# Later batches of a delta-rule scan: each step multiplies by its triangular matrix M itself, and keys and queries are turned by products of 64x64 tiles

## The chip, the cores and the metric

The kernel runs on one core of a Trainium2 chip. The metric is the device time of one execution in microseconds (us); where several executions are shown, their median. Engines are named as in the profile: PE is TensorE's matmul, PEld its weight load, DVE is VectorE, ACT is ScalarE, POOL is GpSimd, SP is SyncE, which issues most DMAs.

## The reference: what is computed

A delta-rule attention runs over 768 time steps for 4 batches of 8 heads with 48 channels; its output, the heads laid side by side (384 channels), goes through a Fourier mixing and a two-layer MLP.

```
for t in range(S):                                   # per batch and head
    y[t]  = q[t] @ state
    v_old = state.T @ kn[t]                          # kn = k / (|k| + 1e-6)
    state = state + beta[t] * outer(kn[t], v[t] - v_old)
x = y, heads side by side                            # (4, 768, 384)
u = x + real(fft(fft(x, axis=seq), axis=channel))
out = u + relu(layernorm(u) @ w1) @ w2               # w1: 384 x 1536, w2: 1536 x 384
```

All of it is float32.

## The kernel before: tiling, staging and the order of the work

Time is cut into chunks of 64 (C). Within a chunk the recurrence is a unit triangular system, so with M the inverse of that triangle (with beta in it) a chunk needs only matrix products: U = M (V - K S), then S' = S + K^T U, and the output Q S + (masked Q K^T) U. Two chunks make a group g of 128 times (L); a batch has 6 groups (NL), the four batches 24. A step is step(g, c) for one chunk c of group g; a batch has 12 of them, one after the other through the state S, for all 8 heads at once.

What does not depend on S is prepared per group, in generators:

- pre_a(g) (line 263) loads a tile C of keys and transposes it to KT: four transposes of 128x128 with TensorE (helper tr, line 106, recorded as L107) into a PSUM tile "one", copied out by ACT (L272). Then the products of KT with itself, and two ACT copies, G and GX (L291, L293).
- invert(r) (line 297) inverts the 32x32 triangles of four groups at once, on DVE: 31 rounds of a multiply (L345) and an add (L349). A round r serves groups 4r to 4r+3.
- pre_q(g) (line 359) transposes the queries to QT in the same way (L371) and forms LQ, the masked product of keys and queries (L389).
- pre_m(g) (line 392) has three parts. POOL scales V by the key norms (L398) and lays out MT (L402), M transposed. Part one: products GX with M (32x32 tiles), ACT copies XM. Part two: products XM with M, ACT copies the last corner of MT (L426). Part three (lines 429 to 446): 16 products of MT with K, which give WT = (M K)^T, and 16 products of MT with V, which give U0 = M V; ACT copies both out (L442, L444).
- step(g, c) (line 448): 8 products of WT with S into a PSUM tile "pair"; DVE subtracts them from U0, which leaves U (L462); 8 products of K with U; DVE adds them to S (L481), which is the next state. With c = 1 it then makes the outputs of the group: 16 products of QT with the two states, copied by ACT (L502), and 16 products of LQ with U, added by DVE (L511).

The PSUM has two tiles "pair" (two banks each), two tiles "one" and two tiles "post" (one bank each), all in rings. In SBUF the rings that matter are V and MT (two each), K (three), and KT (seven, RING).

Batch 0's scan is written out in an order by hand (lines 700 to 775, inside manual_schedule). The scans of batches 1 to 3 (line 776 on) are not: there the program's order gives each instruction only its priority, and the scheduler of the framework puts ready instructions into each engine's queue. That program's order is made by run (line 644), which advances a list of generators by turns: first the step, then pre_q, pre_m and pre_a of later groups, the inversion (six pieces a turn), and then "side", the MLP of the batch before, two pieces a turn and four a step (beside, line 660). A piece of the MLP is three products for a block of hidden units (ph, L104, with a relu on DVE L619 or ACT L617) or four products for an output tile (po). What is left of the MLP after a scan runs beside the Fourier mixing (pf, pb) of the batch just scanned. The MLP of batch 3 has nothing beside it.

A step has a part up to each yield, so before the change: the WT products and the subtraction in the first turn, the K products and the addition in the second, the outputs in the third. The four MLP pieces of a step come in its first two turns.

All products go through mm (line 103, recorded as L104). In the profile one float32 product shows as two MATMUL records (8 calls of the K product are "x16"), a transpose by tr as one ("x4" for a tile).

Of the kernel before, what the change touches and what calls it, by code (L numbers as in the profile page):

```python
# [9 lines left out]
F32 = mybir.dt.float32  # L10
# [3 lines left out]
ALU = mybir.AluOpType  # L14
ACT = mybir.ActivationFunctionType

C = 64
# [41 lines left out]
def kernel(  # L59
# [10 lines left out]
    nc = tc.nc  # L70
# [23 lines left out]
    def ps_pair():  # L94
        return ps.tile([128, 2, 512], F32, tag="pair", bufs=2, name="pair")

    def ps_one():
        return ps.tile([128, 512], F32, tag="one", bufs=2, name="one")
# [4 lines left out]
    def mm(o, lhsT, rhs, start, stop=True):  # L103
        nc.tensor.matmul(o, lhsT=lhsT, rhs=rhs, start=start, stop=stop, skip_group_check=True)  # L104

    def tr(o, src, start):
        nc.tensor.matmul(o, lhsT=src, rhs=ident[0:src.shape[0], 0:src.shape[0]],  # L107
                         is_transpose=True, start=start, stop=True, skip_group_check=True)
# [148 lines left out]
    lo = [slice(64 * e, 64 * e + D) for e in range(2)]  # L257
    full = [slice(64 * e, 64 * e + 64) for e in range(2)]
    KTs, Gs, GXs, rounds, pre, xs = {}, {}, {}, {}, {}, {}
    S = {}  # L260
    SEQ = NL * L

    def pre_a(g):

        K = Cs[g % 3]
        r, li = divmod(g, RL)
        KT = KTs[g] = wk.tile([128, 2, 2, 128], F32, tag="KT", bufs=RING, name="KT")
        pt = ps_one()
        for i in range(4):
            tr(pt[:, 128 * i:128 * i + 128],  # L270
               K[:, 2 * i:2 * i + 2, :].rearrange("p h d -> p (h d)"), i == 0)
        nc.scalar.activation(KT.rearrange("p h j t -> p (h j t)"), pt, ACT.Copy)  # L272
        load_c(g + 3)
        yield
        if li == 0:
            Gs[r] = wk.tile([128, W, W], F32, tag="G", bufs=2, name="G")
        X = GXs[g] = wk.tile([128, 8, W], F32, tag="GX", bufs=8, name="GX")
        pg = ps_pair()
        for i in range(4):
            c, jj = divmod(i, 2)  # L280
            for q4 in range(4):
                for jp in range(2):
                    hh, blk = divmod(q4, 2)
                    t0 = c * C
                    rhs = KT[lo[jp], hh, jj, t0:t0 + C]
                    if blk:
                        rhs = rhs.rearrange("p (b t) -> p b t", b=2)[:, ::-1, :]
                    mm(pg[q4 * W:q4 * W + W, jp, C * i:C * i + C],
                       KT[lo[jp], hh, jj, t0 + blk * W:t0 + blk * W + W], rhs, i == 0)
        src = pg[:, :, 0:4 * C].rearrange("p a (i s) -> p a i s", s=C)  # L290
        nc.scalar.activation(Gs[r][:, 8 * li:8 * li + 8].rearrange("p (i a) s -> p a i s", a=2),  # L291
                             src[:, :, :, 0:W], ACT.Copy)
        nc.scalar.activation(X.rearrange("p (i a) s -> p a i s", a=2), src[:, :, :, W:C],  # L293
                             ACT.Copy)
        yield
# [62 lines left out]

    def pre_q(g, QT=None, LQ=None):

        Q, KT = Qs[g % 2], KTs.pop(g)
        early = QT is not None
        if QT is None:
            QT = wk.tile([128, 2, 2, 128], F32, tag="QT", bufs=2, name="QT")
            LQ = wk.tile([128, 2, 4, C], F32, tag="LQ", bufs=2, name="LQ")
        LQs[g] = (QT, LQ)
        pt = ps_one()
        for i in range(4):
            tr(pt[:, 128 * i:128 * i + 128],
               Q[:, 2 * i:2 * i + 2, :].rearrange("p h d -> p (h d)"), i == 0)  # L370
        nc.scalar.activation(QT.rearrange("p h j t -> p (h j t)"), pt, ACT.Copy)  # L371
        load_q(g + 2)
        yield
        pl = ps_pair()
        for i in range(4):
            c, jj = divmod(i, 2)
            for hh in range(2):
                for jp in range(2):
                    t0 = c * C
                    mm(pl[full[hh], jp, C * i:C * i + C], KT[lo[jp], hh, jj, t0:t0 + C],  # L380
                       QT[lo[jp], hh, jj, t0:t0 + C], i == 0)
        dst = LQ.rearrange("p c (jj jp) t -> p jp (c jj) t", jp=2)
        src = pl[:, :, 0:4 * C].rearrange("p a (i t) -> p a i t", t=C)
        mask = m_su[:, None, None, :].broadcast_to([128, 2, 4, C])
        if early:
            nc.scalar.activation(dst, src, ACT.Copy)
            nc.gpsimd.tensor_tensor(dst, dst, mask, op=ALU.mult)
        else:
            nc.vector.tensor_tensor(dst, src, mask, op=ALU.mult)  # L389
        yield  # L390

    def pre_m(g):

        r, li = divmod(g, RL)
        K, V, X = Ks[g % 3], Vs.pop(g), GXs.pop(g)
        MTd, Md, nT = rounds[r]
        m8 = slice(8 * li, 8 * li + 8)
        nc.gpsimd.tensor_tensor(V.rearrange("p c j d -> p (c j) d"),  # L398
                                V.rearrange("p c j d -> p (c j) d"),
                                nT[:, m8, None].broadcast_to([128, 8, D]), op=ALU.mult)  # L400
        MT = wk.tile([128, 8, 2, W], F32, tag="MT", bufs=2, name="MT")
        nc.gpsimd.tensor_tensor(MT, MTd[:, m8, None, :].broadcast_to([128, 8, 2, W]),  # L402
                                m_blk[:, None, :, None].broadcast_to([128, 8, 2, W]),
                                op=ALU.mult)

        px = ps_one()
        for m in range(8):
            for hh in range(2):
                r0 = 64 * hh
                mm(px[r0 + W:r0 + C, W * m:W * m + W], X[r0:r0 + W, m, :],  # L410
                   Md[r0:r0 + W, 8 * li + m, :], m == 0)
        XM = wk.tile([128, 8, W], F32, tag="XM", name="XM")
        for hh in range(2):
            rw = slice(64 * hh + W, 64 * hh + C)
            nc.scalar.activation(XM[rw].rearrange("p m s -> p (m s)"), px[rw, 0:8 * W],  # L415
                                 ACT.Copy, scale=-1.0)
        yield
        py = ps_one()
        for m in range(8):
            for hh in range(2):  # L420
                r0 = 64 * hh
                mm(py[r0:r0 + W, W * m:W * m + W], XM[r0 + W:r0 + C, m, :],
                   MTd[r0 + W:r0 + C, 8 * li + m, :], m == 0)
        for hh in range(2):
            rw = slice(64 * hh, 64 * hh + W)
            nc.scalar.activation(MT[rw, :, 1, :],  # L426
                                 py[rw, 0:8 * W].rearrange("p (m s) -> p m s", s=W), ACT.Copy)
        yield
        WT = wk.tile([128, 2, 2, 2, C], F32, tag="WT", bufs=2, name="WT")
        U0 = wk.tile([128, 2, 4, D], F32, tag="U0", bufs=2, name="U0")  # L430
        pw = ps_pair()
        pu = ps_one()
        for c in range(2):
            for j in range(4):
                for hh in range(2):
                    mt = MT[full[hh], 4 * c + j].rearrange("p b t -> p (b t)")
                    jj, jp = divmod(j, 2)
                    o = (2 * c + jj) * C
                    mm(pw[full[jp], hh, o:o + C], K[full[hh], 4 * c + j, :], mt, c == 0 and jj == 0)
                    o = (4 * c + j) * D  # L440
                    mm(pu[full[hh], o:o + D], mt, V[full[hh], c, j, :], c == 0 and j == 0)
        nc.scalar.activation(WT.rearrange("p h c j t -> p h (c j t)"), pw[:, :, 0:4 * C],  # L442
                             ACT.Copy)
        nc.scalar.activation(U0.rearrange("p c j d -> p (c j d)"), pu[:, 0:8 * D], ACT.Copy)  # L444
        pre[g] = (K, *LQs.pop(g), WT, U0)
        yield

    def step(g, c):

        b, n = divmod(g, NL)  # L450
        K, QT, LQ, WT, U0 = pre[g]
        begin = n == 0 and c == 0
        s0 = S.get((b, 2 * n + c))
        U = U0[:, c]
        if not begin:
            pw = ps_pair()
            for jj in range(2):
                for hh in range(2):
                    for jp in range(2):
                        mm(pw[full[hh], jp, D * jj:D * jj + D], WT[lo[jp], hh, c, jj, :],  # L460
                           s0[lo[jp], hh, jj, :], jj == 0)
            nc.vector.tensor_tensor(  # L462
                U.rearrange("p (jj jp) e -> p jp jj e", jp=2),
                U.rearrange("p (jj jp) e -> p jp jj e", jp=2),
                pw[:, :, 0:2 * D].rearrange("p a (j e) -> p a j e", e=D), op=ALU.subtract)
            yield
# [354 lines left out]
```

## Time and profile before

| | |
|---|---|
| eight runs | median 829.08 us, 817.48 to 832.37 |
| the profiled execution | 817.48 us, span of the instructions 815.6 us |
| busy in the span | PE 700.1 us, PEld 538.6, DVE 412.6, ACT 203.9, POOL 131.9 |
| batches 1 to 3 and their Fourier parts, 260 to 712 us | PE busy 428.54 of 452 us |
| last MLP, 712 to 816 us | PE busy 97.78 of 104 us |
| mean granted TensorE clock | 0.887 |

"PE busy" counts a matmul from its start to its modelled end, and neighbours overlap, so the cost of a block of products is best read from the start of its first record to the start of the next block's first. A line of the timeline gives the start in us from the span's start, the duration in us, engine, line, operation, output<-inputs, sizes (contraction x stationary columns, then output), and how many records are merged; in brackets, how long the engine was idle before and what released it.

### The profile page before, as it was taken

The numbers are of one execution on the slowest core, as the hardware profiler recorded it, in microseconds if no ns is written. First come the engines' busy times: TensorE is split into PE (matmuls) and PEld (weight loads), VectorE is DVE, ScalarE is ACT, GpSimd is POOL, SyncE is SP. The second block draws the span as 40 slices with busy tenths as digits, with TensorE's granted clock in tenths as the row PEclk, the third lists the DMA queues.
The fourth block names the chain that finished last, engine by engine and source line by source line (L and its number), as shares of the span: only waits on it lengthen the run. The fifth ranks groups of instructions, "written<-read, shape, count | busy, mean of one in ns | idle before, by whom it ended". The sixth has DMA issues, their size and how long they took to land.

```text
span 815.6 us, 23216 instructions
## 1 busy us (share of the span) xinstructions
PE 700.1 (86%) x10344; PEld 538.6 (66%) x10344; DVE 412.6 (51%) x1004; ACT 203.9 (25%) x470; POOL 131.9 (16%) x150
## 2 busy tenths in 40 slices
PE   5537565398888999899998898899999999899998
PEld 4426464387657767578866767677778677686774
DVE  1897757546997129926268414798122141611110
ACT  4312333163322422023312213212122121210010
POOL 6132135302311101132000102102000020100000
PEclk8555555596999999999998999999999999899999
DMA  9721144323300421112111122002010000000000
GB/s 133 210 44 27 32 104 111 94 42 86 114 16 21 75 52 34 23 31 55 32 37 31 21 45 46 12 10 46 17 45 17 11 12 1 19 1 20 10 10 19
DMA packets 107382, 36.06 MB, mean 44 GB/s; under 512 B 99633, under 2 KB 102930, under 8 KB 107282
## 3 DMA queue, kind: packets, MB, share of 16 engines
q1 hardware_dynamic: 105586, 33.50, 18.4%
q8 instruction: 81, 1.33, 0.7%
q0 software_dynamic: 512, 0.79, 0.6%
q10 hardware_dynamic: 1184, 0.30, 0.3%
q14 instruction: 19, 0.16, 0.1%
HBM read 29.84 MB, written 4.72 MB: 42 GB/s over the span
## 4 chain that ended last, share of the span: by engine, by line
PE 54%; DVE 30%; issue 5%; POOL 4%; ACT 3%; DMA 2%; SPq 1%; ACTq 0%; POOLq 0%; DVEq 0%
PE po L104 17%; PE ph L104 16%; PE pair L104 8%; DVE M L349 6%; DVE tmp L345 6%; PE one L104 5%; PE pf L104 3%; PE one L107 2%; PE pb L104 2%; DMA C<-in_k_dram 2%; POOL w L246 1%; DVE A L304 1%; DVE A L352 1%; DVE G L353 1%; DVE hT L619 1%
## 5 line engine op out<-in xcount | busy, mean ns | idle before, releaser
L104 PE MATMUL ph<-unT,w 128*128 128x256 f32 x864 | 209.2, 396 | 9.6 <-DVE hT L619 5.9
L104 PE MATMUL po<-w,hT 128*128 128x384 f32 x576 | 198.1, 496 | 5.6 <-POOL w L246 3.1
L104 PEld LDWEIGHTS ph<-unT,w 128*128 128x128 f32 x864 | 164.6, 196 | 37.7 <-DVE hT L619 9.1
L104 PEld LDWEIGHTS po<-w,hT 128*128 128x128 f32 x576 | 108.3, 192 | 74.0 <-POOL w L246 3.2
L619 DVE TENSOR_SCALAR hT<-ph 128x256 f32<-128x256 f32 x72 | 30.3, 421 | 109.6 <-PE ph L104 109.6
L349 DVE TENSOR_TENSOR M<-M,tmp 128x135 f32<-128x135 f32 (+15 forms) x186 | 71.5, 386 | 4.8
L345 DVE TENSOR_TENSOR tmp<-A,M 128x60 f32<-128x60 f32 (+15 forms) x186 | 69.5, 375 | 4.4
L617 ACT ACTIVATE hT<-ph 128x256 f32<-128x256 f32 x72 | 27.6, 384 | 145.4 <-PE ph L104 142.3
L629 DVE TENSOR_TENSOR x<-x,po 128x384 f32<-128x384 f32 x24 | 13.2, 551 | 97.3 <-PE po L104 97.2
L104 PE MATMUL one<-V,MT 64*64 64x48 f32 x768 | 47.4, 241 | 0.9 <-ACT MT L426 0.8
L402 POOL TENSOR_TENSOR MT<-A,pack 128x512 f32<-128x512 f32 x24 | 26.1, 1094 | 131.0 <-PE one L104 79.1
L398 POOL TENSOR_TENSOR V<-V,nT 128x384 f32<-128x384 f32 x24 | 20.8, 869 | 155.5 <-DMA V<-in_v_dram 55.1
L104 PEld LDWEIGHTS one<-V,MT 64*64 64x64 f32 x768 | 43.2, 159 | 2.8 <-ACT MT L426 1.7
L104 PE MATMUL pair<-MT,K 64*64 64x64 f32 x768 | 42.3, 256 | 1.6 <-ACT MT L426 1.0
L104 PE MATMUL pair<-S,WT 48*64 48x48 f32 x704 | 22.6, 245 | 21.7 <-DVE S L481 17.4
L104 PEld LDWEIGHTS pair<-MT,K 64*64 64x64 f32 x768 | 38.4, 151 | 3.2 <-ACT MT L426 1.6
L104 PEld LDWEIGHTS pair<-S,WT 48*64 48x64 f32 x704 | 16.7, 151 | 31.1 <-DVE S L481 18.6
L104 PEld LDWEIGHTS pair<-U,K 64*64 64x64 f32 x704 | 16.9, 151 | 30.4 <-DVE U L462 15.3
L104 PE MATMUL pair<-U,K 64*64 64x48 f32 x704 | 23.2, 246 | 15.4 <-DVE U L462 13.8
L481 DVE TENSOR_TENSOR S<-S,pair 128x192 f32<-128x192 f32 x40 | 14.0, 349 | 37.2 <-PE pair L104 37.2
L104 PE MATMUL one<-G,GX 32*32 32x32 f32 x768 | 19.0, 204 | 15.2 <-DVE G L353 15.2
L415 ACT ACTIVATE XM<-one 32x256 f32<-32x256 f32 x48 | 18.1, 376 | 54.6 <-PE one L104 53.6
(111 smaller groups left out, 923.4 us busy)
## 6 DMA issues: line engine op xcount, KB each, us to landing
w<-in_moe_w_ch_dram SPq DMA_DIRECT2D x12, 768.0 KB
Q<-in_q_dram SPq DMA_DIRECT2D x24, 192.0 KB
out_dram<-x SPq DMA_DIRECT2D x24, 192.0 KB
C<-in_k_dram SPq DMA_DIRECT2D x23, 192.0 KB
K<-in_k_dram SPq DMA_DIRECT2D x88, 48.0 KB
V<-in_v_dram SPq DMA_DIRECT2D x88, 48.0 KB
evt<-k_even SPq DMA_DIRECT2D x1, 579.0 KB
odt<-k_odd SPq DMA_DIRECT2D x1, 576.0 KB
```

The source lines that it names most:

```text
L104: nc.tensor.matmul(o, lhsT=lhsT, rhs=rhs, start=start, stop=stop, skip_group_check=True)
L107: nc.tensor.matmul(o, lhsT=src, rhs=ident[0:src.shape[0], 0:src.shape[0]], is_transpose=True, start=start, stop=True, skip_group_check=True)
L246: nc.gpsimd.tensor_tensor(dst, man.rearrange("p (c f) -> p c f", c=c), num.bitcast(F32).rearrange("p (c f) -> p c f", c=c), op=ALU.mult)
L345: nc.vector.tensor_tensor(t, A[:, j + 1:W, j:j + 1].broadcast_to([128, n, j + 1]), M[:, j:j + 1, 0:j + 1].broadcast_to([128, n, j + 1]), o ...
L349: nc.vector.tensor_tensor(M[:, j + 1:W, 0:j + 1], M[:, j + 1:W, 0:j + 1], t, op=ALU.add)
L398: nc.gpsimd.tensor_tensor(V.rearrange("p c j d -> p (c j) d"), V.rearrange("p c j d -> p (c j) d"), nT[:, m8, None].broadcast_to([128, 8, ...
L402: nc.gpsimd.tensor_tensor(MT, MTd[:, m8, None, :].broadcast_to([128, 8, 2, W]), m_blk[:, None, :, None].broadcast_to([128, 8, 2, W]), op=A ...
L415: nc.scalar.activation(XM[rw].rearrange("p m s -> p (m s)"), px[rw, 0:8 * W], ACT.Copy, scale=-1.0)
L481: nc.vector.tensor_tensor(s1v, s0.rearrange("p h j e -> p h (j e)"), pk, op=ALU.add)
L617: nc.scalar.activation(hT[:, fc, :], ph, ACT.Relu)
L619: nc.vector.tensor_scalar(hT[:, fc, :], ph, 0.0, None, op0=ALU.max)
L629: nc.vector.tensor_tensor(x[:, T, :], x[:, T, :], po, op=ALU.add)
```

## The change

Four things change, the first three only for batches 1 to 3 (groups 6 to 23).

1. pre_m ends after its second part: the 32 products of MT with K and V and the two ACT copies (WT, U0) are gone. What is handed to the step is MT and V.
2. A step of those batches multiplies KT with S (8 products, as many as WT with S before), DVE subtracts from V in place, then 8 products of MT with the difference give U in a PSUM tile "one", and ACT copies U out. Only then come the products of K with U. A step thus has one more turn: the four MLP pieces stand in the turns of KT S and of M, and K U with the addition stands in a third turn by itself.
3. KT, MT and V of a group are now read by the group's steps, so their ring buffers are held until the step of chunk 1 has read them.
4. For all 24 groups, keys and queries are turned by a new helper, turn: in place of four 128x128 transposes into "one", 16 plain products of 64x64 tiles with the identity into a "pair" (one bank for each half of the partitions), and one ACT copy of the same 512 elements a partition.

```diff
+    def turn(dst, src):
+
+        pt = ps_pair()
+        for i in range(4):
+            for c in range(2):
+                for jp in range(2):
+                    nc.tensor.matmul(pt[full[jp], c, C * i:C * i + C],
+                                     lhsT=src[full[c], 2 * i + jp, :], rhs=ident[full[c], full[c]],
+                                     start=i == 0, stop=True,
+                                     skip_group_check=True)
+        nc.scalar.activation(dst.rearrange("p h j (c t) -> p c (h j) t", c=2),
+                             pt[:, :, 0:4 * C].rearrange("p c (i t) -> p c i t", t=C), ACT.Copy)
...
-        pt = ps_one()
-        for i in range(4):
-            tr(pt[:, 128 * i:128 * i + 128],
-               K[:, 2 * i:2 * i + 2, :].rearrange("p h d -> p (h d)"), i == 0)
-        nc.scalar.activation(KT.rearrange("p h j t -> p (h j t)"), pt, ACT.Copy)
+        turn(KT, K)
...
-        Q, KT = Qs[g % 2], KTs.pop(g)
+        Q, KT = Qs[g % 2], KTs[g]
...
+        turn(QT, Q)
...
+        if g >= NL:
+            pre[g] = (K, *LQs.pop(g), MT, V)
+            yield
+            return
...
+        if b > 0:
+
+            if c == 0:
+                Us[0] = wk.tile([128, 2, 4, D], F32, tag="U0", bufs=2, name="U")
+            K, QT, LQ, MT, V = pre[g]
+            U0, KT = Us[0], KTs[g]
+            R, U = V[:, c], U0[:, c]
+            if not begin:
+                pw = ps_pair()
+                for jj in range(2):
+                    for hh in range(2):
+                        for jp in range(2):
+                            mm(pw[full[hh], jp, D * jj:D * jj + D],
+                               KT[lo[jp], hh, jj, c * C:c * C + C], s0[lo[jp], hh, jj, :], jj == 0)
+                R4 = R.rearrange("p (jj jp) e -> p jp jj e", jp=2)
+                nc.vector.tensor_tensor(
+                    R4, R4, pw[:, :, 0:2 * D].rearrange("p a (j e) -> p a j e", e=D),
+                    op=ALU.subtract)
+                yield
+            pu = ps_one()
+            for j in range(4):
+                for hh in range(2):
+                    mm(pu[full[hh], D * j:D * j + D],
+                       MT[full[hh], 4 * c + j].rearrange("p b t -> p (b t)"), R[full[hh], j, :],
+                       j == 0)
+            nc.scalar.activation(U.rearrange("p j e -> p (j e)"), pu[:, 0:4 * D], ACT.Copy)
+            yield
+        else:
+            K, QT, LQ, WT, U0 = pre[g]
+            U = U0[:, c]
+        if not begin and b == 0:
```

More of the change, by code (lines that the diff above doesn't have):

```diff
@@ L259 @@
     KTs, Gs, GXs, rounds, pre, xs = {}, {}, {}, {}, {}, {}
-    S = {}
+    S, Us = {}, {}
     SEQ = NL * L
+    def turn(dst, src):
[9 more added lines that the diff above has]
+                             pt[:, :, 0:4 * C].rearrange("p c (i t) -> p c i t", t=C), ACT.Copy)
     def pre_a(g):
@@ L366, in pre_q @@
         LQs[g] = (QT, LQ)
[L367 to L371, printed above, removed]
+        turn(QT, Q)
         load_q(g + 2)
@@ L450, in step @@
         b, n = divmod(g, NL)
-        K, QT, LQ, WT, U0 = pre[g]
         begin = n == 0 and c == 0
         s0 = S.get((b, 2 * n + c))
-        U = U0[:, c]
-        if not begin:
+        if b > 0:
[28 more added lines that the diff above has]
+        if not begin and b == 0:
             pw = ps_pair()
```

## The prediction

> **What bounds the kernel now.** I read the page first (engines, then the 40 slices), then the busy times by stage, then PE's timeline inside the stages, and last the waits of PE.
>
> ```profile
> PE 700.1 (86%) x10344; PEld 538.6 (66%) x10344; DVE 412.6 (51%) x1004; ACT 203.9 (25%) x470; POOL 131.9 (16%) x150
> PE   5537565398888999899998898899999999899998
> DVE  1897757546997129926268414798122141611110
> ```
>
> PE is low in the first third and at eight or nine tenths from slice 13 on (about 250 us): batches 1 to 3, where the change sits, are held mostly by PE. But DVE has three humps there. The busy times by stage (columns: length, then PE, PEld, DVE, ACT, POOL busy with counts, clock, DMA) separate them:
>
> ```profile
> 260.00:303.00 43.00, 42.60 (x986) 31.50 (x984) 6.63 (x16) 14.90 (x35) 4.73 (x6) 1.00 0.28 57
> 303.00:348.00 45.00, 38.79 (x573) 28.42 (x565) 42.34 (x109) 8.28 (x21) 7.63 (x8) 0.96 0.16 30
> ...
> 413.00:456.00 43.00, 38.59 (x549) 27.64 (x550) 37.13 (x96) 7.92 (x19) 3.95 (x5) 0.92 0.17 35
> ...
> 517.00:566.00 49.00, 44.88 (x358) 34.88 (x357) 44.96 (x127) 10.52 (x30) 4.78 (x8) 1.00 0.10 23
> 566.00:660.00 94.00, 92.98 (x1517) 68.50 (x1516) 20.61 (x47) 21.02 (x49) 7.58 (x8) 1.00 0.10 24
> ```
>
> Three stretches, 137 us together, belong to an inversion on DVE, with 4 to 6 us of PE idle in each: PE work saved there is no time. Between them PE is busy for 42.60 of 43 and 92.98 of 94 us. There each microsecond of PE work counts, and each wait that nothing fills. PE's timeline in the last stretch shows the repeating order:
>
> ```profile
> 610.42 0.45 PE L104 MATMUL pair<-U,K 64*64 64x48 f32 x16
> 612.23 2.86 PE L104 MATMUL ph<-unT,w 128*128 128x256 f32 x12
> 615.02 0.68 PE L104 MATMUL pair<-S,QT 48*64 48x48 f32 x32
> 615.52 0.65 PE L104 MATMUL pair<-U,LQ 64*64 64x48 f32 x32
> 616.31 0.45 PE L104 MATMUL pair<-S,WT 48*64 48x48 f32 x16
> 617.28 0.69 PE L104 MATMUL one<-G,GX 32*32 32x32 f32 x32
> 617.90 2.86 PE L104 MATMUL ph<-unT,w 128*128 128x256 f32 x12
> 620.69 0.45 PE L104 MATMUL pair<-U,K 64*64 64x48 f32 x16
> 620.96 0.66 PE L104 MATMUL pair<-QT,KT 48*64 48x64 f32 x32
> 621.55 2.86 PE L104 MATMUL ph<-unT,w 128*128 128x256 f32 x12
> 624.34 0.45 PE L104 MATMUL pair<-S,WT 48*64 48x48 f32 x16
> ```
>
> After the first product of each step (S,WT) and after its second (U,K) come two MLP pieces (ph, 2.8 us): DVE's subtraction or addition is done behind them, and PE waits for nothing. In PE's waits from 260 to 712 us the state (S L481) accounts for 2.0 us and U (L462) for 0.8 us.
>
> **The change part by part**, against the profiled execution's 817.48 us.
>
> 1. *Part three of pre_m goes.* Its 64 records run from 409.09 to 410.72 us, up to the next block: 1.63 us. Of the 18 groups, two (6 and 7) come before 260 us, where DVE holds the end (19.18 of 20 us busy from 240 to 260), and three of the other 16 fall into inversion stretches. 13 x 1.63 = -21.2 us. The ACT copies (0.60 + 0.48 us) were hidden behind PE, and so is their going.
>
> 2. *M in the step.* The new 8 products have the form of the MT,V products, 64x64 on 48 columns, and use only two of the four 64x64 places in the array. Where those ran apart from the MT,K products the trace has their price:
>
> ```profile
> 380.06 0.90 PE L104 MATMUL one<-V,MT 64*64 64x48 f32 x22
> 380.88 0.55 PE L107 MATMUL ptr<-pack,un 128*128 128x128 f32 x3
> ```
>
> 22 records in 0.82 us, less about 0.11 for the change of form (below), are 32 ns each; 16 are 0.52 us. Other bound: U,K, 16 records on all four places, 0.27 us (620.69 to 620.96). Upper bound: 0.52 and 0.11, 0.63. I take 0.53, the same products. The 13 groups have 26 steps: +13.8 us. So what the change saves on PE is mainly the MT,K half of part three.
>
> 3. *The turns.* 4 transposes take 0.49 us from their start to the next block (446.57 to 447.06, queries). 16 products of 64x64 on 64 columns are 32 records; QT,KT has that form: 0.59 us up to ph (620.96 to 621.55); S,QT, as many on 48 columns, takes 0.50 before a block of its own form. But QT,KT goes over the four places with the row half changing each time, turn takes both column halves of one row half before it changes; part three does too and cost 1.63/64 = 25 ns a record, so 0.81 us is the upper bound. The trace does not show turn's order; QT,KT's form is nearest. 27 turns lie after 260 us; 0.59 - 0.49 on some, and nothing where a block of the same form precedes (S,WT before transposes costs 0.38 us, U,K before QT,KT 0.27: a change of form is 0.11): I take +0.04 each, +1.1 us, bounds -1 and +8.6. In the first 60 us, at the lower clock, 4 transposes take 1.04 us (20.47 to 21.51) and QT,KT 1.06 (35.88 to 36.94): equal, and mostly beside DVE's first inversions. ACT's copy keeps its 512 elements (WT's copy out of a "pair" is 0.60 us, like KT's out of a "one"): nothing.
>
>    [...]
>
> 4. *Order.* K U now stands in a turn without MLP pieces, and the next step's KT S follows it. The scheduler may fill that place with other blocks (A,XM, 32x32) or a piece of MLP, at two more changes of form: 13 x 2 x 0.11 = +2.9 us, bounds 0 and 5.7 (every step).
>
> 5. *Waits.* The chain of a step grows by one link: subtraction, M product, ACT copy, K product. The subtraction is covered by two MLP pieces, and so is the ACT copy (0.35 us by DVE's same 192 elements, 0.48 by U's copy of 384): nothing, while the pieces last. Without cover a link costs what this shows:
>
> ```profile
> 388.78 0.45 PE L104 MATMUL pair<-U,K 64*64 64x48 f32 x16
> ...
> 389.32 0.35 DVE L481 TENSOR_TENSOR S<-S,pair 128x192 f32<-128x192 f32 x1
> ...
> 389.73 0.70 PEld L104 LDWEIGHTS pair<-KT 48*32 48x32 f32 x64 [0.16 <-DVE S L481]
> ```
>
>    From the start of U,K to PE released by the addition: 0.95 us, of which U,K itself is 0.27. So with c = 0, where K U and the next KT S are neighbours, up to 0.68 us each; with c = 1 the 32 output products stand between, but their second "pair" waits for the addition (0.95 - 0.27 - 0.51 = 0.17), and the turn of the next queries, now in a "pair" too, waits for the output's addition on DVE (L511, at 512.25 us after U,LQ at 511.47, end 512.81; PE is free about 1.05 after U,LQ's start: 0.3). 11 x 0.68 + 11 x 0.47 = 12.7 us if nothing fills. The scheduler has ready blocks to put there, as it put ptr between records of U,K at 300.38 us. I take a quarter: +3.2.
>
> 6. *Rings.* V and MT are held until step(g, 1) has read them, so the loads of V for g + 2 and POOL's MT start up to two steps later. Four issues take 2.58 us (411.19), a landing 5.7, POOL 0.83 + 1.04: 10.2 us, against 2.5 steps of about 9 us up to their use. Queued behind: on POOL the Fourier sums (L528), on ACT the copies into MT and, behind them, relus. Cover: the steps' own length. Without it 1 to 2 us a group. I take 0. On SP only loads and stores queue, due steps later: nothing. KT's ring of seven frees each buffer at least one step before its next writer.
>
> Sum: -21.2 + 13.8 + 1.1 + 2.9 + 3.2 + 0 = -0.2 us, 817.3 for an execution like the profiled one. That one was the fastest of eight, 11.6 us under their median; the sum is a difference, so I put it on the median: 829.08 - 0.2, about **829**.
>
> **The rivals.**
>
> *Faster: everything new is filled.* For it: PE waits hardly at all in these stretches now, and the scheduler works with ready instructions. Then terms 4 and 5 vanish and the M products overlap somewhat (0.40 in place of 0.53): -21.2 + 10.4 + 1.1 = -9.7, 819 us. Against it: MT,V cost 32 ns apart and no less inside part three.
>
> *Slower: the place behind K U stays bare.* One mechanism: the addition to S is done behind K U, nothing is put between, PE idles 0.68 us after chunk 0 and 0.47 after chunk 1. Price 12.7 in place of 3.2, and then with the changes of form at their bound: -0.2 + 9.5 + 2.8 = +12.1, 841 us. It decides from about 8 us (1%) more idle than in the sum, where two thirds of these places stay bare. For it: DVE also has the inversion's pieces queued, six a turn, so the addition can come 2.3 us late (U,K at 426.31, addition at 428.88). Against it: those stretches already have PE idle.
>
> *Turn at 25 ns a record.* +7.5 on the sum, 836 to 837: still within 1% alone, slower with any of the bare waits.
>
> *It doesn't save what it removes,* because PE's saved work lies where DVE holds the end: then the saving shrinks to nothing and 3 to 5 us of waits are left, 833.
>
> **How the numbers follow.** About 1% (8.3 us) is what a measurement here can tell from no change. Near-cancellation, with the fourth rival and half of the third: 0.40, 822 to 837, likeliest 829. Slower (bare places, alone or with dear turns, or late V): 0.35. Faster: 0.25. Low end: all of the first rival and a little of U,K's price for M: 816. High end: bare places with turns at 25 ns would be 849; a tenth is left out there: 845.
>
> **What the profile after would show.** PE busy from the start of batch 1 to the last MLP down by 5 to 9 us; blocks "one<-V,MT"-like of 16 records at 0.5 us in each step; turns of 32 records at 0.5 to 0.65 us (0.8 would make term 3 wrong); between K U and the next KT S a filled block (term 4) or PE idle released by S's addition (term 5, the slower rival); POOL waiting for V's DMA less than 3 us longer in a group (else term 6 is wrong). The prediction is wrong if PE idle in 260 to 712 us grows by over 10 us, or if DVE's three stretches get longer because subtractions and inversion collide.

## The result, and the profile after

The changed kernel takes 834.14 us (median of 19 runs, 828.36 to 842.08); the kernel before 827.04 (median of 56 runs). The ratio is 1.0112, 95% interval 1.0086 to 1.0139: slower by about 1%, 7 to 9 us, where -0.2 us was forecast. The ratio is taken over the fast executions of each kernel, those within 1.5% of its fastest; the medians of all executions give 1.0086. The time lies in the range, the sum does not hold.

The page of the changed kernel, its engines and PE's slices:

```profile
PE 709.7 (86%) x11112; PEld 545.5 (66%) x11112; DVE 413.2 (50%) x1004; ACT 199.2 (24%) x470; POOL 135.0 (16%) x150
PE   4636565687889998899989998899999999899998
```

PE has 768 records more and 9.6 us more busy time. By stage (columns as before the change):

```profile
258.00:307.00 49.00, 47.93 (x1119) 36.23 (x1120) 7.89 (x18) 14.37 (x36) 5.38 (x6) 0.90 0.27 53
307.00:351.00 44.00, 37.78 (x590) 28.30 (x591) 41.70 (x108) 7.86 (x20) 7.28 (x8) 0.93 0.16 29
524.00:575.00 51.00, 46.44 (x430) 36.62 (x431) 46.01 (x132) 11.54 (x33) 6.59 (x9) 0.97 0.08 19
575.00:674.00 99.00, 98.61 (x1519) 71.90 (x1517) 25.68 (x55) 20.68 (x51) 12.40 (x14) 1.00 0.12 27
```

The pattern of the stages is that of before: DVE's inversions in the second and third line, PE in the others. Two things differ. The clock in the first line is 0.90 (it was 1.00), but a second execution of the kernel before has 0.92 from 260 to 303 us, so this alone tells nothing of the change. And PE has a new wait.

```profile
PE pair L269 <- DVE x L548: 6.2, 5, 3.1
PE pair L104 <- DVE S L518: 5.2, 4, 2.0
```

The first is the turn (L269): its PSUM tile is now a "pair", and the tile before it in that ring is the one that holds the group's outputs until DVE has added them to x (L548). The second is the addition to S, 2.0 us before the change.

### The profile page after: what moved, and what is told of

Same layout as the page of the kernel before. It is cut to its first block, busy times and chain, and to the rows that moved or that the text cites. A ratio compares the mean times of both kernels' runs of the same rounds, so it can differ in the third digit from the quotient of the medians.

```text
span 828.6 us, 24829 instructions
## 1 busy us (share of the span) xinstructions
PE 709.7 (86%) x11112; PEld 545.5 (66%) x11112; DVE 413.2 (50%) x1004; ACT 199.2 (24%) x470; POOL 135.0 (16%) x150
## 4 chain that ended last, share of the span: by engine, by line
PE 58%; DVE 26%; issue 5%; POOL 5%; ACT 3%; DMA 1%; SPq 1%; DVEq 0%; ACTq 0%; POOLq 0%
PE po L104 19%; PE ph L104 17%; PE pair L104 8%; DVE tmp L354 5%; PE one L104 5%; DVE M L358 5%; PE pf L104 4%; PE pair L269 3%; POOL w L246 2%; DVE A L313 1%; PE pb L104 1%; POOL E L566 1%; PE ptr L107 1%; POOL E L565 1%; DVE hT L656 1%
## 5 line engine op out<-in xcount | busy, mean ns | idle before, releaser
L104 PE MATMUL ph<-unT,w 128*128 128x256 f32 x864 | 213.1, 399 | 4.5 <-ACT unT L645 3.1
L358 DVE TENSOR_TENSOR M<-M,tmp 128x135 f32<-128x135 f32 (+15 forms) x186 | 68.7, 371 | 4.7
L104 PEld LDWEIGHTS one<-V,MT 64*64 64x64 f32 x768 | 37.1, 160 | 14.1 <-issue 10.8
L104 PE MATMUL one<-V,MT 64*64 64x48 f32 x768 | 43.0, 247 | 0.5 <-issue 0.5
L104 PEld LDWEIGHTS pair<-U,K 64*64 64x64 f32 x704 | 17.0, 153 | 26.3 <-DVE U L499 13.2
L104 PE MATMUL pb<-dtab,F 97*128 97x97 f32 (+1 forms) x192 | 27.7, 292 | 6.9 <-DVE x L615 5.7
L104 PE MATMUL pair<-KT 48*32 48x64 f32 x1536 | 24.0, 254 | 9.4 <-issue 8.0
L104 PEld LDWEIGHTS pb<-dtab,F 97*128 97x128 f32 (+1 forms) x192 | 25.3, 202 | 9.9 <-issue 4.2
L269 PE MATMUL pair<-pack,Q 64*64 64x64 f32 x768 | 21.8, 259 | 11.7 <-DVE x L548 6.2
L431 ACT ACTIVATE MT<-one 32x256 f32<-32x256 f32 x48 | 18.0, 374 | 48.5 <-PE one L104 45.4
L269 PE MATMUL pair<-pack,C 64*64 64x64 f32 x768 | 22.7, 269 | 6.9 <-DMA C<-in_k_dram 5.5
```

What stands on the lines that cost most here:

```text
L269: nc.tensor.matmul(pt[full[jp], c, C * i:C * i + C], lhsT=src[full[c], 2 * i + jp, :], rhs=ident[full[c], full[c]], start=i == 0, stop=Tru ...
L358: nc.vector.tensor_tensor(M[:, j + 1:W, 0:j + 1], M[:, j + 1:W, 0:j + 1], t, op=ALU.add)
L431: nc.scalar.activation(MT[rw, :, 1, :], py[rw, 0:8 * W].rearrange("p (m s) -> p m s", s=W), ACT.Copy)
```

## The experiments

Eleven more kernels ran, and four of the kernels once more for a second profile. Two theories stood against each other. A: the turns of keys and queries lose the time (records, the ring "pair", and the clock behind PE's gaps). B: the step's longer chain and V's later loads lose it.

**The parts by themselves.** M alone puts the transposes back, in both places, into the changed kernel:

```diff
-        turn(KT, K)
+        pt = ps_one()
+        for i in range(4):
+            tr(pt[:, 128 * i:128 * i + 128],
+               K[:, 2 * i:2 * i + 2, :].rearrange("p h d -> p (h d)"), i == 0)
+        nc.scalar.activation(KT.rearrange("p h j t -> p (h j t)"), pt, ACT.Copy)
```

> The changed kernel with keys and queries transposed as before (four 128x128 transposes into a "one"), so the steps' multiplication by M alone. Theory A (the turns lose the time: a turn costs 0.63 us in place of 0.49, stands in a "pair" and waits for the output's addition, and each gap halves the granted clock for some us): 824 to 829 us, ratio to the kernel before 0.990 to 1.000. Theory B (the longer chain of the step and the later loads of V lose it): 833 to 837 us, ratio 1.005 to 1.013, no faster than the changed kernel.

The turn alone is the kernel before with turn(KT, K) and turn(QT, Q):

> The kernel before with the new turn of keys and queries alone; part three of pre_m and the steps are as before. Theory A: 833 to 840 us, ratio 1.008 to 1.016, and PE waits in the turn for the output's addition or stands idle just before turns. Theory B: the 27 turns at +0.14 us add about 4 us at most, ratio 1.000 to 1.005.

M alone: 817.57 us, ratio 0.9894 (0.9798 to 0.9991). The turn alone: 832.55, ratio 1.0123 (1.0067 to 1.0180). A expected 0.990 to 1.000 and 1.008 to 1.016: the turn alone falls there, M alone is a little faster still, and both lie far from what B expected. So the change consists of a gain of about 1% by M and a loss by the turns, of 1.2% on the kernel before and about 2% on M alone.

**A third buffer for V**, first in the changed kernel, then with M alone:

```diff
-            Vs[g] = wk.tile([128, 2, 4, D], F32, tag="V", bufs=2, name="V")
+            Vs[g] = wk.tile([128, 2, 4, D], F32, tag="V", bufs=3, name="V")
...
-        WT = wk.tile([128, 2, 2, 2, C], F32, tag="WT", bufs=2, name="WT")
+        WT = wk.tile([128, 2, 2, 2, C], F32, tag="WT", bufs=1, name="WT")
```

> The changed kernel with three buffers for V in place of two (and one for WT, which only batch 0 uses), so that V's load for group g + 2 no longer waits for the M product of group g. Theory A: within 2 us of the changed kernel (833 to 836, ratio 1.009 to 1.013). Theory B: 3 to 8 us less than the changed kernel (826 to 831), POOL's wait for V's DMA gone, and with it the 3 us gaps of PE near 503 and 532 us.

> Transposes as before, M in the steps, and three buffers for V: the first and the third of these runs together. Theory A: as the run with M alone (824 to 829). Theory B: about 828, 5 us less than the run with M alone. If both theories hold half: 820 to 825, less than the kernel before.

826.55 (ratio 1.0028, 0.9983 to 1.0072) and 813.56 (0.9899, 0.9845 to 0.9953). The first fits B's numbers, and its interval lies apart from the changed kernel's; the second gives no gain over M alone by the ratios (813.56 against 817.57 by the times). B's place fits only in part. The additions to S in batch 0, which the change of the steps does not touch, already come 1.2 to 2.4 us earlier from the fourth on (90.38 to 88.64 us in the changed kernel, 88.73 to 86.82 with M alone): V's buffers were short in batch 0 all along. POOL's waits for V's DMA after 257 us, which B expected to go, are 57.3 us with the third buffer, 37.3 and 65.5 in two executions of the changed kernel, 45.7 and 47.4 in two of the kernel before. As the cause of the whole loss B fails, for M alone has its longer chain and its later loads and is faster than the kernel before. But the late V has a part in one long wait, shown further down, and the rest of the third buffer's 7 us in the changed kernel stays open.

**Which of the turn's properties costs?** The transposes into a "pair" (pt = ps_pair()[:, 0, :] in place of ps_one(), nothing else), then keys alone and queries alone turned by products:

> M in the steps and keys and queries transposed as before, but into a "pair" in place of a "one": only the ring of the PSUM buffer is that of the change, the instructions are those of before. If sharing the ring "pair" costs the time (the transposes then wait for the output's addition): ratio to the kernel before 1.003 to 1.010, PE waiting 4 us or more on that addition. If the 32 records of a turn cost it by their own duration: as with M alone, 0.985 to 0.995.

> The changed kernel with the queries transposed as before into a "one"; only keys are turned by products. In the profile of the turn alone all waits of a turn for the output's addition were in turns of queries. If these waits cost the time: close to M alone, ratio 0.988 to 0.996. If a turn costs its records, half of what both lose: 0.998 to 1.003.

> The changed kernel with the keys transposed as before; only queries are turned by products. If the waits of the queries' turns cost the time: close to the changed kernel, ratio 1.006 to 1.012. If a turn costs its records: 0.998 to 1.003, as with keys alone.

The ring alone: 826.31, ratio 0.9992 (0.9949 to 1.0036), between the two forecasts. By the ratios it takes back most of M's gain with the instructions of before, though its interval overlaps with that of M alone. Keys: 823.21, 0.9966 (0.9933 to 0.9998). Queries: 824.09, 0.9979 (0.9939 to 1.0019). My sharper reading, that only the queries' waits cost, is not borne out: by the ratios keys cost as much as queries. Where keys cost, the next experiment shows.

**The first 30 us.** Only the keys of the first eight groups turned by products (if g < 2 * RL: turn(KT, K), else the transposes), with M in the steps:

> M in the steps and only the keys of the first eight groups turned by products, all other keys and all queries transposed as before. If the first turns cost PE's stops at the start (it reaches the same count of records sooner, and stops once or twice more): 2 to 3 us later than M alone from the first step on, stops of 8 us or more in all, ratio about 0.993. If these turns were beside the first inversions, as forecast: no later than M alone, ratio 0.988 to 0.991.

823.28 us, ratio 0.9982 (0.9938 to 1.0026). The first addition to S starts at

```
without turned keys   before 70.2, 70.4   M alone 70.9, 70.4   ring alone 70.6, 71.0   queries 69.9
with turned keys      after 72.7, 72.9    turn alone 72.4      keys 72.7               first eight keys 73.8
```

(two numbers are two executions). PE's timeline shows a reason. M alone:

```profile
11.13 1.09 PE L104 MATMUL pair<-KT 48*32 48x64 f32 x77
15.58 0.74 PE L104 MATMUL pair<-KT 48*32 48x64 f32 x51 [3.36 <-issue]
```

The changed kernel:

```profile
9.85 0.94 PE L104 MATMUL pair<-KT 48*32 48x64 f32 x61
12.61 0.30 PE L104 MATMUL pair<-KT 48*32 48x64 f32 x3 [1.82 <-issue]
...
18.73 0.85 PE L104 MATMUL pair<-KT 48*32 48x64 f32 x36 [3.43 <-issue]
...
28.84 0.43 PE L104 MATMUL pair<-KT 48*32 48x64 f32 x6 [2.75 <-issue]
```

PE stops and waits for nothing that the profile shows. The first stop comes after the same 221 matmul records in both kernels (the counts added up from the start; give or take one, it is 221 in all seventeen profiles). With turns of 32 records in place of 4 PE gets there sooner and meets the next stops too, after 348 and 602 records, in every profile with turned keys. M alone passes these counts later, at 21.7 and 36.6 us, and does not stop. Over the whole span such stops make 8.6 to 12.8 us in six executions with turned keys, 2.2 to 4.9 in ten without. DVE's first inversion waits for these keys: it starts at 16.78 us with M alone and at 20.03 in the changed kernel. Of these 3.3 us the stops before it make 1.9 (5.25 in place of 3.36 us); the rest lies between the blocks and is not divided. The delay stays to the end of batch 0's additions, at 1 to 3 us. The ratio expected was 0.993. The profiled execution has the PE work and idle of M alone behind 257 us, within 1.5 us, and lost more to half clock (13.0 us between 257 and 355 us, against 3.4 and 9.7 in two executions of M alone); whether that holds for the median of twelve is not shown.

**Second profiles**, kernels unchanged:

> The kernel before, unchanged, for a second profile: its executions lie between 815 and 832 us, and the profiled one was among the fastest. If executions of one kernel differ by when the clock falls to a half, an execution that is N us longer shows about N us more of PE work at half clock, with the same waits in the same places; if not, the clock is the same and waits or transfers are longer.

> M alone, unchanged, for a second profile. If its gain over the kernel before is PE's own work and the start of batch 1: the same landmarks before 257 us as in its first profile (3 us ahead of the kernel before) and a time lost at half clock that alone explains the difference between its two executions. If its gain is a lucky clock: a time of 825 us or more.

> The changed kernel, unchanged, for a second profile. Stops of PE that wait for nothing the profile shows, near 12, 18 and 28 us, come again and total 8 us or more if they belong to the keys' turns; 2 to 4 us as in the kernels with transposes if they are chance. Waits of the queries' turns for the output's addition come again at the same places.

> Transposes as before but into a "pair", unchanged, for a second profile. In the first, PE's work and idle after 256 us were those of M alone within 1.5 us, and 14 us more were lost at half clock. If the ring itself sets the clock: again 24 us or more lost after 230 us. If that was one execution's chance: 12 to 22, as in the other kernels, and the step-to-step times from 580 to 676 us again 0.5 us longer than with M alone.

They took 826.64, 821.17, 832.57 and 824.26 us. The two executions of the kernel before have all additions to S at the same times within 0.4 us until 250 us. The distance then grows in two stretches, from 250 to 268 us (+3.0) and from 503 to 569 us (+6.7), and changes nowhere else by more than 0.4. The larger part of the second; the faster execution, then the other, over the same instructions:

```profile
554.47:569.49 15.02, 14.68 (x237) 12.24 (x239) 11.93 (x33) 4.52 (x12) 2.81 (x5) 1.00 0.27 53
```

```profile
558.90:578.95 20.05, 20.05 (x238) 17.32 (x241) 11.59 (x33) 4.63 (x12) 2.80 (x5) 0.67 0.20 40
```

The same work between the same two additions, and 5 us more at a granted clock of 0.67. So a profile must be split before two kernels are compared. I cut PE's time from the end of inversion 2 (the G that follows it, near 257 us) to PE's end into slices of 2 us: idle; lost, which is busy time times one minus the granted clock; and work, the rest of busy.

```
us                   until G         work            idle          lost
before               257.8, 257.7    515.5, 513.9    27.9, 29.0    11.0, 20.8
M alone              254.4, 254.3    513.5, 511.8    28.3, 27.9    12.5, 22.2
ring alone           255.7, 256.2    512.3, 512.8    27.6, 29.9    26.3, 20.1
after                256.6, 258.2    517.8, 517.8    30.3, 30.7    20.4, 20.5
keys / queries       259.4 / 253.5   514.0 / 514.4   28.5 / 27.3   18.8 / 24.2
```

The first three columns repeat to about 2 us, the last moves by up to 10 us from one execution of a kernel to the next. The ring's 24 us or more at half clock did not come again (20.1 after 26.3): what sets it stays open. From the means of the pairs the turns (after less M alone) cost +3.1 until G, +5.2 work, +2.4 idle and +3.1 at half clock, this last within chance. For M only the sum of the first three columns can be compared, for G does not stand at the same step: when it starts, the kernel before has begun four steps of batch 1, M alone and all others of this table three. The sums:

```
before 801.2, 800.6   M alone 796.2, 794.0   ring alone 795.6, 798.9   after 804.7, 806.7   keys 801.9   queries 795.2
```

M gives -5.8, the turns +10.6, together +4.8; the other 4.6 us of the 9.4 by which the two profiles of the changed kernel are longer is half clock. That the 9.4 agree with 9.3 by the ratio is therefore in part luck. Keys alone add 6.8 us to M alone and queries alone 0.1, in one execution each, where the ratios put them level; how the 10.6 divide between them is not shown.

**One stretch that PE holds alone, clock 1.00.** From the start of the second U,K of batch 3 to that of the eleventh (last), nine steps with four turns of queries:

```
before 93.54, 93.51   M alone 93.64, 93.63   keys 93.64   ring alone 94.18, 94.17   queries 94.58   after 94.58, 94.58
```

Both ends lie on PE. The additions to S would mislead here, for in the kernel before the last one stands behind Fourier sums on DVE and starts 2.44 us after its U,K (0.52 with M alone):

```profile
662.49 0.45 PE L104 MATMUL pair<-U,K 64*64 64x48 f32 x16
...
664.93 0.34 DVE L481 TENSOR_TENSOR S<-S,pair 128x192 f32<-128x192 f32 x1
```

M gains nothing in this stretch (+0.1), though the kernel before has 288 records of part three in it and one block of transposes less. The turns of queries cost +0.94, which is 0.24 us each; 0.13 of it comes with the ring alone. The timeline of M alone, then that of the changed kernel, at the same step:

```profile
590.91 0.45 PE L104 MATMUL pair<-S,KT 48*64 48x48 f32 x16
591.28 0.66 PE L107 MATMUL one<-pack,Q 128*128 128x128 f32 x4
591.87 0.69 PE L104 MATMUL one<-G,GX 32*32 32x32 f32 x32
592.50 5.43 PE L104 MATMUL po<-w,hT 128*128 128x384 f32 x16
```

```profile
606.32 0.45 PE L104 MATMUL pair<-S,KT 48*64 48x48 f32 x16
606.70 0.63 PE L104 MATMUL one<-G,GX 32*32 32x32 f32 x28
607.26 0.69 PE L269 MATMUL pair<-pack,Q 64*64 64x64 f32 x32
607.88 0.25 PE L104 MATMUL one<-G,GX 32*32 32x32 f32 x4
608.06 5.43 PE L104 MATMUL po<-w,hT 128*128 128x384 f32 x16
```

From S,KT to po 1.59 us become 1.74. In a "pair" the turn must wait for the outputs' addition, so the scheduler puts it behind most of G,GX, into the middle of a block of another form. Over the four turns of the stretch, from each block's start to the next block's: the transposes take 2.41 us with M alone, where one block of four is cut in two, 2.25 in the ring "pair", the turns 2.50; the four G,GX take 2.49, 2.84 and 2.84, in the last two with three of them cut in two. So a turn's records cost 0.06 us more than transposes in the same place, and of the 0.94 us the ring makes 0.54. Where DVE is late the same wait is bare:

```profile
502.03 0.63 PE L104 MATMUL one<-G,GX 32*32 32x32 f32 x28
505.79 1.13 PE L269 MATMUL pair<-pack,Q 64*64 64x64 f32 x32 [3.12 <-DVE x L548]
```

```profile
505.79:512.00 6.21, 6.21 (x77) 5.19 (x78) 5.41 (x12) 2.33 (x5) 2.27 (x2) 0.51 0.17 34
```

PE idles 3.12 us until x is added, and the next 6 us run at a clock of 0.51. The wait goes back further. DVE itself stands for 3.68 us, until POOL has made a Fourier sum (E), and POOL has just stood for V:

```profile
501.95 0.83 POOL L403 TENSOR_TENSOR V<-V,nT 128x384 f32<-128x384 f32 x1 [4.02 <-DMA V<-in_v_dram]
...
503.69 0.99 POOL L566 TENSOR_TENSOR E<-x 128x384 f32<-128x384 f32 x1
...
504.71 0.56 DVE L569 TENSOR_TENSOR O<-E 128x382 f32<-128x382 f32 x1 [3.68 <-POOL E L566]
505.19 0.55 DVE L548 TENSOR_TENSOR x<-x,pair 128x384 f32<-128x384 f32 x1
```

With the third buffer for V, POOL makes these sums before it scales V, and the turns' waits for x fall from 6.2 and 5.8 us to 2.7, the longest from 3.1 and 3.2 to 1.1. This long wait stands, at 2.3 to 3.4 us, in all seven profiles that have M, two buffers for V and turns or transposes into a "pair" at this place, and neither in the turn alone nor in M alone. So it takes both, the ring "pair" and the late V.

**Prices by doubling.** The M products issued twice (for j in [0, 1, 2, 3] * 2, with M alone and three buffers for V), and the products of the turn issued twice in the changed kernel:

> M in the steps, transposes as before, three buffers for V, and each of the 8 M products issued twice (the second overwrites the first with the same values): the price of the M product itself. By the sum's 0.53 us on the 26 steps that PE holds: 14 us more than without, 827 to 829, ratio 1.000 to 1.006. If the products lie beside other work: under 5 us more, ratio below 0.996. If the change of form were most of the price: 7 us more.

> The changed kernel with the 16 products of each turn issued twice (the second overwrites the first with the same values): the price of a turn's records themselves. At the 0.6 us of a turn in the trace on the 27 turns after 260 us: 16 us more than the changed kernel, and about 1 us more for each of the first eight turns, 850 to 856, ratio 1.028 to 1.036. If the records lie beside other work and only the place of the turn costs: under 5 us more, ratio below 1.018.

The M products: 822.80, ratio 1.0004 (0.9949 to 1.0059), 8.7 us more by the ratios. In the trace a block of 16 records takes 0.60 us to the next block, one of 32 takes 1.07: 0.47 for 16 records and 0.13 that does not grow with them. In the stretch above the nine steps take 3.9 us longer, 0.43 each. So the price of 0.53 lies between 0.47 without the change of form and 0.60 with it. 26 steps at 0.47 are 12.2 us; the 8.7 by the ratios are less, and their interval is as wide as they are. The turns: 867.34, ratio 1.0484 (1.0407 to 1.0561), 31 us more than the changed kernel, where I expected 16 behind 260 us and some 8 before. A turn of 64 records takes 1.09 us against 0.62, so 27 of them explain 13 us behind 260 us; 10 more lie before it (inversion 2 ends at 267.7 in place of 256.6 and 258.2). Of the rest 7 us are PE's idle behind 257 us (37.7 in place of 30.3 and 30.7), whose waits I have not followed.

**One MLP piece in each turn of a step** (part(side, want - done), 1 in place of 2, on M with three buffers for V):

> M in the steps, transposes as before, three buffers for V, and one piece of the MLP in each turn of a step (KT S, M, K U, outputs) in place of two in each of the first two. If the bare place behind K U and the waits for the addition to S cost time (5.9 us of PE idle in the profile of M alone): those waits under 2 us and a ratio of 0.983 to 0.988. If a single piece of 1.4 us is too short to cover the subtraction or the copy: more waits, ratio 0.990 to 1.000.

812.31, ratio 0.9897 (0.9855 to 0.9938), no different from 0.9899 without. PE's waits for the addition to S are gone (5.7 us without), and in the nine steps of batch 3 PE idles 0.00 in place of 0.46 us; but these steps take 94.09 us in place of 93.63. What covering the bare place behind K U saves in waits it costs in work. This, M with three buffers for V (813.56) and M alone are the versions that beat both kernels, by about 1% in ratio.

## Why the prediction was wrong, point by point

- *Step 3, the turns: the step that failed.* It put +0.04 us on each of 27 turns, +1.1 in all, with bounds -1 and +8.6. Measured against M alone: +5.2 work, +2.4 idle and +3.1 until inversion 2's end, 10.6 us, before any clock. Three parts of it were wrong. The difference in price between 32 records and four transposes was about right (+0.06 in the same place). But the sum left the turns in the transposes' places; the ring moved them into the middle of G,GX, and in the nine steps of batch 3 each costs 0.24 net. Next, "equal, and mostly beside DVE's first inversions" for the first 60 us: equal in duration, yes, but not in records, and PE's stops go by records (the first after 221 in all seventeen profiles): the first addition to S comes 2 to 3 us later, on the path of the first inversion. Last, the wait for the output's addition, which step 5 priced at 0.3 us, is up to 3.2 us where DVE has the inversion's or the Fourier pieces queued before it, the longest of them together with V's late load.
- *The upper bound in step 3, 25 ns a record.* From part three's 1.63/64 it made 0.81 us a turn and +8.6 us in all. The turns show 17 to 19 ns a record (0.62 us for 32, 1.09 for 64), so this price does not hold here; its sum came nearer to the 10.6 us for reasons that are not in it.
- *Steps 1, 2 and 4, part three against the M product and the order.* Together -4.5 us after 260 us were forecast. In the nine steps of batch 3, which PE holds, the terms give -7.3 (288 records of part three at 1.63/64) + 4.8 + 1.0, and +0.5 for one more block of transposes: -1.0. Measured: +0.1. So a step with M cost about 0.12 us more than the sum had it; 0.07 of this is the product, 0.60 us to the next block in place of 0.53. That M alone is nevertheless 5.8 us shorter must come from elsewhere. The forecast left out groups 6 and 7, which it put where "DVE holds the end"; but inversion 2 ends at least 3.3 us earlier in each of five profiles of M with transposes (251.4 to 254.4 us; V's ring is the larger one in three of them). That the part three of these two groups does it is likely, but not shown.
- *Step 5, waits.* +3.2 were forecast. PE's wait for S grew from 2.0 to 5.9 us with M alone, but its idle as a whole did not (28.5 before, 28.1 with M alone, means of two): other waits went. The sign set for it, over 10 us more PE idle from 260 to 712 us, did not come (23.5 us before, 23.7 after).
- *Step 6, rings: 0.* The steps' length does not cover V's load everywhere: POOL's 4 us for V lie behind the turn's longest wait, and in the changed kernel a third buffer is worth 1 to 3 us in the sums of the split (804.0 in one execution, 804.7 and 806.7 without) and 7 us by the ratios. MT's ring alone was not tried.
- *The rivals.* "The place behind K U stays bare" came on the right side and for the wrong reason: covering the place gains nothing. "It doesn't save what it removes" came nearest, 833 for 834.14, by chance: M alone does save, and the turns lose it again. "Turn at 25 ns a record" named the right part, at a price that the turns do not show (17 to 19 ns). "Everything new is filled" has the number of M alone, 819 for 817.57, but not its way: it has the M products at 0.40 us and no waits; they cost 0.47 to 0.60, and PE's wait for S grew.

What stays open: how much of the ring's 1% is its own. The sums of the split give 2 us; the rest is time at half clock, which one execution more or less shifts by 6 us.

## What to carry to other kernels

Ask of a moved or replaced block not only how long it takes, but which buffer ring it writes to and who empties the tile before: here a block of the same length in another ring took another place in PE's order, and paid a change of form on both sides (the ring made 0.54 us in nine steps with four blocks) and the waits of that ring (up to 3.2 us). At a kernel's start count PE's records, not only their time: the first stop here came after 221 records in every profile. Measure a stretch between two blocks of the engine that holds it, and count that both kernels have the same work between them. And before two profiles are compared, split PE's time into work, idle and time at half clock: the third differed here by up to 10 us between executions of one program, so two profiles do not show what a kernel adds to it.

## What the runs showed of the hardware that I had not expected

- Half clock comes in pieces. In seventeen profiles there are 130 stretches at 0.50 between 230 us and PE's end; each lasts some 3.4 us or a multiple, and most lose 1.5 to 1.7 us of PE time or a multiple of it (3.4, 5.1, 6.8, 10.2). Each begins inside a gap of PE of 0.35 us or more, or at most 2.7 us behind its end, and such places make up only 14% of this time. Short gaps were followed by it too: in the kernel before, a gap of 1.08 us at 704.24 is followed by 4.5 us lost from 706 to 717. But of 183 gaps of 1 us or more only 100 are followed by half clock. The gap of 2.3 us at 257 us is followed by nothing in one execution of that kernel and by 3.4 us lost in the other.
- PE's stops after 221, 348, 602 and 856 matmul records, 127 or 254 apart. In the changed kernel they last 1.82, 3.43, 2.75 and 0.59 us; the longest is 4.11 us, after 602 records, in the changed kernel with a third buffer for V. What makes PE stop at these counts is not shown.
- A block of 16 records on two diagonal places of the array costs 29 ns a record (0.47 us for the 16 that the doubled M products add); the turn's records, 64x64 on all four, cost 15 ((1.09 - 0.62) us for 32).
